# One departure of TensorE per chunk, attention one batch ahead, and a pinned TensorE order

## The chip, the cores and the metric

The program runs on one NeuronCore of a Trainium2 chip. The metric is the device time of one execution in microseconds. The engines are named as in the profile: PE is TensorE, DVE VectorE, ACT ScalarE, POOL GpSimd, SP the engine that issues most DMAs.

## The reference

Eight batches, eight heads, 576 positions, head dimension 64. Three layers follow each other; all of it is float32.

```python
# 1 Nystrom attention, m = 32 landmarks (means of 18 positions)
A, Bm, C = sm(q, k_lm), sm(q_lm, k_lm), sm(q_lm, k)      # softmax of scaled products
Z = Bm.T / (norm1(Bm) * norminf(Bm) + 1e-6)
for _ in range(6): Z = 2*Z - Z @ Bm @ Z                  # inverse of Bm by iteration
x = A @ Z @ C @ v                                        # 4608 tokens x 512
# 2 gated layer: 512 -> 1536 -> 512
x = (silu(x @ w_gate) * (x @ w_val)) @ w_out
# 3 soft mixture of experts, 8 experts x 4 slots
logits = x @ phi
slots  = softmax(logits, over tokens).T @ x
out    = softmax(logits, over slots) @ expert(slots)     # expert: relu(s @ w1) @ w2
```

## The kernel before

**The main loop.** It goes over the 8 batches, and in a batch over 12 chunks `j` of 128 gate columns: 96 chunks. Softmax matrix A stands transposed in SBUF as a high and a low part (EH, EL), and Z C v is folded with the weights into `g`, again as GH and GL. A chunk is 24 matmuls at line 903 (`mm3`): for each half of the positions six into the bank `pg` (gate) and six into `pv` (value). This text calls these 24 the stream. ACT makes `u` of `pg` (silu, L301, or tanh, L917), DVE multiplies `u` and `pv` into `hT` (L932) and transposes `hT` into HB (L761).

**The other matmuls stand between them.** All are plain float32 (the stream is float32r), and most use the array in smaller tiles than the stream's 128*128 (a row names the tile; `m_n`, `m_t` and `m_ps` have 128*128 too): `l`, the logits of the chunk before (L756, 8 records); `g` for two chunks (L710, 16 records; one chunk in batches 0 and 7 and at the end of batch 6), which ACT casts to GH (L727) and DVE subtracts to GL (L741); for the attention of the next batch the landmark sums on DVE (L322), the scores `m_a` of A and `m_c` of C (L529, 16 records for each half), transposes `m_t` (L596, L601), `m_v` (L618), six steps `m_n` of the inverse (L637) and the product `m_w` (L522); for the slots of the batch before `m_dr`, which spreads the weights DN over the row groups (L841), and the slot sums `m_d` (L872, 144 records), added to Sacc by DVE (L882). A row of the profile counts two records for each such matmul.

A stretch of such matmuls between two of the stream is called a departure here.

**What sets their order.** `slot(i)` in `unit` is called four times a chunk (after each six of the stream), so a batch has 48 slots. The lists in SCHED (`at*` attention, `am*` softmax of A, `sm` soft mixture) say in which slot each step of a generator is written, numbers below zero belonging to the batch before. A scheduler then orders the instructions of each engine, and may move a matmul past others. PSUM is shared: three banks `x` for nearly everything beside the stream, two `pg`, two `pv`, one `l`. `in_order` keeps exponentials and silus of ACT in written order, so that tables change twice in a batch; chunks named in TANH use tanh, whose table is that of the exponential.

After the loop the slots go through the experts, whose weights are loaded from batch 7 on, and the output is written.

Of the kernel before, what the change touches and what calls it, by code (L numbers as in the profile page):

```python
# [8 lines left out]
F32 = mybir.dt.float32  # L9
# [44 lines left out]
def nystrom_softmoe_kernel(  # L54
# [286 lines left out]
    def attention_tiles(b):  # L341
        ks = ap.tile([128, 4, M], F32, tag="ks", name="ks")
        qs = ap.tile([128, 4, M], F32, tag="qs", name="qs")
        if b != 1:
            e_tiles(b)
# [3 lines left out]
        return ks, qs, AN, CE  # L349

    def first_attention(side):
        b = 0
        ks, qs, AN, CE = attention_tiles(b)
        NBUF = big("w5", "newton").rearrange("p (i q m) -> p i q m", q=2, m=128)
# [177 lines left out]
    def attention(b):  # L532
        assert b == 1 or ("att", b - 1) in seq
        ks, qs, AN, CE = attention_tiles(b)
        for nm, dst in (("k", ks), ("q", qs)):
            for hp in range(4):
# [3 lines left out]
                yield  # L540
        for half in range(2):
            ms = [psp.tile([128, 512], F32, tag="x", name="m_a", bufs=3) for r in range(2)]
            scores(ms, ks, "q", b, half, range(4))
            assert b == 1 or ("asm", b - 1) in seq
            seq.add(("A", b, half))
            for r in range(2):
                dve.transpose(AN[r][:, 9 * half:9 * half + 9, :], ms[r][:, 0:HALF].rearrange("p (t r) -> p t r", r=32))
                yield
        for half in range(2):
            ms = [psp.tile([128, 512], F32, tag="x", name="m_c", bufs=3) for r in range(2)]  # L550
            scores(ms, qs, "k", b, half, range(4))
            n = HALF
            if half:
                n += M
                for hp in range(4):
                    for r in range(2):
                        pe.matmul(ms[r][32 * hp:32 * hp + 32, HALF:n], qs[64 * r:64 * r + 64, hp, :],
                                  ks[64 * r:64 * r + 64, hp, :], start=True, stop=True)
            for r in range(2):
                act.copy(CE[r][:, HALF * half:HALF * half + n], ms[r][:, 0:n])  # L560
                yield
        if b == 1:
# [101 lines left out]
    def a_softmax(b, qs=(0, 1)):  # L664
        EH, EL = E_t[b]
        AN, mxA = A_t[b]
# [125 lines left out]
    def softmoe(b):  # L792
# [96 lines left out]
        yield  # L889
        dve.tensor_reduce(mx, c, axis=AX.X, op=ALU.add)  # L890
        dve.tensor_scalar(mx, mx, 1e-9, None, ALU.add)
        dve.reciprocal(mx, mx)
        dve.tensor_tensor(out=c, in0=c, in1=bc, op=ALU.mult)
        yield
# [11 lines left out]
    def unit(b, j, slot):  # L906
# [118 lines left out]
    def tail_loads(b, n):  # L1025
# [19 lines left out]
    for a in range(1, nb):  # L1045
# [4 lines left out]
        sm = softmoe(a - 1)  # L1050
        for r in S_["sm"]:
            todo[48 * a + r].append(sm)
    prev = None
    for b in range(nb):
        for j in range(NJ):
            p = prev
            def slot(i):
# [29 lines left out]
                if n == 47:  # L1087
# [211 lines left out]
```

## Time and profile before

| | us |
|---|---|
| median of 3 runs | 687.33 (687.18 to 689.19) |
| profiled execution, its own time | 688.07 |
| its span | 686.3 |
| PE busy | 641.6 (93%) |
| DVE busy | 484.5 (71%) |
| ACT busy | 307.2 (45%) |
| POOL busy | 72.2 (11%) |

The profiled execution is 0.74 us above the median and 1.77 us longer than its span. Busy PE is not PE at work: a matmul that waits inside the array counts. So stretches are measured here from the start of one instruction to the start of another. Batch 0 takes 85.5 us of the loop, in which the weights are prepared too; batches 1 to 6 take 68 to 70 us each, batch 7 57.6 us, and the part after the loop some 85 us. In the stretches of batches 1 to 7 the granted clock is 1.00, that is 2.4 GHz.

### The profile page before, as it was taken

What the parts mean: (1) busy time and instruction counts of PE and PEld (TensorE: products, weight loads), DVE (VectorE), ACT (ScalarE), POOL (GpSimd) and SP (SyncE); (2) the same over time, 40 slices, a digit from 0 to 9 for tenths busy, and PEclk for the clock granted to TensorE, in tenths of its full rate; (3) what the DMA queues carried; (4) which work ended last, traced back from release to release, by engine and by line L of the source; (5) the groups of instructions that cost most, each with busy time, mean ns of one, the idle gap of its engine ahead of it and who ended that gap; (6) DMA issues with size and microseconds to landing.
All of it is one profiled execution on the core that took longest, in us unless ns stands there. A gap on an engine that the chain in (4) does not pass through costs nothing.

```text
span 686.3 us, 18326 instructions
## 1 busy us (share of the span) xinstructions
PE 641.6 (93%) x7639; PEld 470.2 (69%) x7639; DVE 484.5 (71%) x1166; ACT 307.2 (45%) x776; POOL 72.2 (11%) x81
## 2 busy tenths in 40 slices
PE   5699999999999999999999999999999999989991
PEld 2576767776877687777777777777768886843560
DVE  4999989878657985798569856976696655550441
ACT  2566875356335533463246324632364342321441
POOL 0401012012001200120012001200130000010000
PEclk9799999999999999999999999999999999999996
DMA  7788773232203230224022402240212296789999
GB/s 283 258 323 316 279 269 119 83 126 84 70 1 96 72 114 2 72 82 126 1 71 71 140 1 70 72 139 1 71 63 63 77 367 227 249 268 351 348 369 326
DMA packets 59843, 105.01 MB, mean 153 GB/s; under 512 B 3824, under 2 KB 29552, under 8 KB 58224
## 3 DMA queue, kind: packets, MB, share of 16 engines
q1 hardware_dynamic: 59760, 103.84, 45.0%
q8 instruction: 60, 0.98, 0.6%
q14 instruction: 23, 0.19, 0.1%
HBM read 91.24 MB, written 12.58 MB: 151 GB/s over the span
## 4 chain that ended last, share of the span: by engine, by line
PE 68%; DVE 17%; ACT 6%; DMA 4%; issue 2%; POOL 1%; SPq 0%; POOLq 0%; ACTq 0%; DVEq 0%
PE pg L903 20%; PE pv L903 17%; PE g L710 6%; PE l L756 4%; PE m_n L637 3%; PE m_d L872 3%; PE m_f L1232 2%; PE m_f L1184 2%; PE m_a L529 2%; DMA q<-in_qT_dram 2%; DMA v<-in_v_dram 2%; DVE bd L311 2%; DVE GL L741 1%; DVE Sacc L882 1%; DVE qs L322 1%
## 5 line engine op out<-in xcount | busy, mean ns | idle before, releaser
L301 ACT ACTIVATE u<-pg 128x288 f32<-128x288 f32 x174 | 71.4, 411 | 143.8 <-PE pg L903 138.7
L932 DVE TENSOR_TENSOR hT<-u,pv 128x288 f32<-128x288 f32 x174 | 78.2, 450 | 56.9 <-PE pv L903 51.3
L903 PE MATMUL pg<-EH,GH 128*128 128x288 f32 x384 | 96.9, 330 | 2.5 <-ACT GH L727 1.6
L741 DVE TENSOR_TENSOR GL<-g,GH 128x512 fp32r<-128x512 f32 (+1 forms) x122 | 66.0, 571 | 38.7 <-ACT GH L727 38.5
L903 PE MATMUL pv<-EH,GH 128*128 128x288 f32 x384 | 91.2, 312 | 0.5 <-DVE hT L932 0.5
L903 PE MATMUL pg<-EH,GL 128*128 128x288 f32 x384 | 86.0, 299 | 0.0
L903 PE MATMUL pg<-EL,GH 128*128 128x288 f32 x384 | 84.0, 298 | 0.0
L903 PE MATMUL pv<-EH,GL 128*128 128x288 f32 x384 | 83.1, 295 | 0.0
L903 PE MATMUL pv<-EL,GH 128*128 128x288 f32 x384 | 82.7, 296 | 0.0
L727 ACT CAST GH<-g 128x512 fp32r<-128x512 f32 (+1 forms) x122 | 54.2, 496 | 56.4 <-PE g L710 56.3
L903 PEld LDWEIGHTS pg<-EH,GH 128*128 128x128 f32 x384 | 59.9, 189 | 25.3 <-issue 20.3
L761 DVE STREAM_TRANSPOSE HB<-hT 128x576 f32<-128x576 f32 x96 | 73.9, 770 | 1.3
L903 PEld LDWEIGHTS pv<-EH,GH 128*128 128x128 f32 x384 | 61.4, 188 | 18.0 <-issue 16.2
L903 PEld LDWEIGHTS pg<-EH,GL 128*128 128x128 f32 x384 | 62.3, 188 | 2.2 <-issue 2.1
L903 PEld LDWEIGHTS pg<-EL,GH 128*128 128x128 f32 x384 | 61.6, 188 | 1.8 <-issue 1.8
L903 PEld LDWEIGHTS pv<-EL,GH 128*128 128x128 f32 x384 | 61.6, 188 | 0.9 <-issue 0.9
L903 PEld LDWEIGHTS pv<-EH,GL 128*128 128x128 f32 x384 | 61.9, 188 | 0.5 <-issue 0.5
L710 PE MATMUL g<-w,WB 64*32 64x512 f32 (+1 forms) x976 | 56.5, 510 | 0.4 <-ACT WB L523 0.4
L756 PE MATMUL l<-hT,P_sb 128*32 128x128 f32 (+1 forms) x768 | 47.4, 298 | 0.7 <-DVE hT L932 0.6
L756 PEld LDWEIGHTS l<-hT,P_sb 128*32 128x32 f32 x768 | 15.9, 108 | 40.3 <-issue 17.8
L872 PE MATMUL m_d<-HB,HB 32*32 32x384 f32 x1116 | 39.5, 491 | 0.3 <-DVE GL L741 0.3
L683 POOL TENSOR_TENSOR AN<-AN,mxA 128x576 f32<-128x576 f32 x16 | 18.4, 1170 | 179.6 <-DVE mxA L682 163.3
(248 smaller groups left out, 945.2 us busy)
## 6 DMA issues: line engine op xcount, KB each, us to landing
k<-in_kT_dram SPq DMA_DIRECT2D x52, 288.0 KB, 3.8
ffn<-in_w_dram SPq DMA_DIRECT2D x13, 1024.0 KB, 8.7
ffn<-in_w_dram SPq DMA_DIRECT2D x24, 512.0 KB, 8.8
HB<-in_w_cat_dram SPq DMA_DIRECT2D x8, 1024.0 KB, 7.8
v<-in_v_dram SPq DMA_DIRECT2D x8, 1024.0 KB, 6.0
q<-in_qT_dram SPq DMA_DIRECT2D x28, 288.0 KB, 3.2
HB<-in_w_out_dram SPq DMA_DIRECT2D x12, 512.0 KB, 5.8
wr<-in_w_cat_dram SPq DMA_DIRECT2D x4, 1024.0 KB, 9.4
```

Source lines behind the costliest of these rows:

```text
L301: i = act.activation(*a, **kw)
L311: dve.tensor_tensor(out=dst[:, q, :].rearrange("p (h m) -> p h m", h=4), in0=src.unsqueeze(1).to_broadcast([128, 4, 32]), in1=bm3, op=ALU. ...
L637: pe.matmul(m[:, 96 * q:96 * q + 96], bd[:, q, :], RV[:, q, :], start=True, stop=True)
L683: lambda q: pool.tensor_tensor(out=AN[q], in0=AN[q], in1=bc[q], op=ALU.subtract),
L710: pe.matmul(gs[r][32 * hp:32 * hp + 32, 0:256 * n].rearrange("p (u f) -> p u f", u=n), WB[b % 2][64 * r:64 * r + 64, hp, :], w[64 * r:64 * ...
L727: act.copy(H_, g)
L741: dve.tensor_tensor(out=GL, in0=g, in1=GH, op=ALU.subtract)
L756: pe.matmul(L[32 * c:32 * c + 32, 0:32 * k], P_sb[:, j, :], main[:, 0:k, c, :], start=j == 0, stop=j == NJ - 1)
L761: dve.transpose(HB[b % 2][:, S * j:S * j + S].rearrange("p (t r) -> p t r", r=32), hT[:, 0:S].rearrange("p (t r) -> p t r", r=32))
L872: pe.matmul(ms[a][32 * g:32 * g + 32, 0:384].rearrange("p (j f) -> p j f", j=NJ), d_of(a, g, k), hb[32 * a:32 * a + 32, :, 4 * k + g, :], ...
L903: pe.matmul(ps[:, 0:HALF], G_t[b, j, q, sel_][h], e[:, q, ts_], start=n == 0, stop=n == 5)
L932: dve.tensor_tensor(out=o, in0=u, in1=pv[:, 0:HALF], op=ALU.mult)
```

## The change

- The scores of A for all four tiles (two halves, two rows of heads) are issued together, so too those of C; they take one bank `pv` and the three `x` (from batch 2 on, `together`).
- Attention of batch b+1 begins in batch b-1 (`at3`, `am3`): landmark sums in its slots 29 to 40, scores of A in slot 41; the rest follows in batch b. The tiles EH and EL are asked for later, where A is transposed back.
- The steps are put into slots 4j+1, in which the logits stand.
- DN is spread by 12 small DMAs on SP in place of four matmuls and four copies, for batches 0 to 5.
- `keep_order` ties each PE instruction from batch 1 on to the one written before it.
- The tanh chunks are others (three halves of a batch as before); the first `g` of a batch stands one slot earlier; two fences hold a few DVE reductions back.

```diff
-    'at3': [-3, -2, -1, 0, 3, 4, 5, 6, 8, 8, 10, 10, 16, 16, 18, 18, 19, 20, 20, 21, ...
+    'at3': [-19, -18, -17, -16, -11, -10, -9, -8, -7, -6, -6, -5, 1, 2, 2, 3, 4, 5, 5, 6, ...
-    'sm': [1, 3, 10, 17, 19, 20, 23, 24, 24, 27],
+    'sm': [1, 2, 3, 6, 7, 7, 25, 26, 26, 28],
...
+    def keep_order(engine, start, end):
+        last = None
+        for i in nc.cur_bb.bb.instructions[start:end]:
+            if i.engine == engine:
+                if last is not None:
+                    tc.add_manual_dep(i, last.name, mybir.DependencyInfo(
+                        mybir.DependencyClass.NoSync, mybir.DependencyReason.DATA), reason="keep_order")
+                last = i
...
+        def score_tiles(name):
+            ms = [psp.tile([128, 512], F32, tag="pv" if i == 3 else "x", name=name, bufs=2 if i == 3 else 3)
+                  for i in (3, 0, 1, 2)]
+            return {(1, 1): ms[0], (0, 0): ms[1], (0, 1): ms[2], (1, 0): ms[3]}
...
+            if together:
+                t = score_tiles(name)
+                for half in (1, 0):
+                    product(half, [t[half, 0], t[half, 1]])
+                for half, r in ((1, 1), (0, 0), (0, 1), (1, 0)):
+                    eviction(half, r, t[half, r])
+                    yield
...
-            for g in range(4):
+            for i in range(1, 4 if b < nb - 2 else 1):
+                for a in range(4):
+                    sp.dma_start(DR[32 * a:32 * a + 32, a ^ i], DN[32 * (a ^ i):32 * (a ^ i) + 32])
+            for g in range(4 if b == nb - 2 else 0):
                 m = psp.tile([128, 512], F32, tag="x", name="m_dr", bufs=3)
...
-            d_of = lambda a, g, k: DR[32 * a:32 * a + 32, g, k, :]
+            d_of = lambda a, g, k: (DN if a == g else DR[:, g])[32 * a:32 * a + 32, k, :]
...
-    TANH = {(4, 1), (5, 0), (5, 1)}
+    TANH = [{(5, 0), (5, 1), (6, 0)}, {(1, 1), (2, 0), (2, 1)}]
...
-                if n == 46 and b + 1 < nb:
+                if n == (46 if b == 0 else 45) and b + 1 < nb:
                     g_unit(b + 1, 0)
...
+    keep_order(mybir.EngineType.PE, middle, n_ins())
```

By the built programs, PE leaves the stream 227 times in the loop before and 139 times with the change; in each of batches 2 to 5 it is 28 times and 12 times.

On PE, the end of batch 3 before (`pg` and `pv` are the stream; inverse step, product `m_w`, logits, `g` of the next batch):

```order
L637 MATMUL m_n<-RV,bd 128x96 x2
...
L522 MATMUL m_w<-bd,VD 64x128 x2
...
L756 MATMUL l<-hT,P_sb 32x160 x2
L756 MATMUL l<-hT,P_sb 32x128 x2
...
L710 MATMUL g<-w_214,WB_75 32x512 x8
...
L756 MATMUL l<-hT,P_sb 32x160
L903 MATMUL pg<-EH,GL 128x288
L903 MATMUL pv<-EH,GL 128x288
L756 MATMUL l<-hT,P_sb 32x160
L756 MATMUL l<-hT,P_sb 32x128 x2
```

With the change the same place reads:

```order
L945 MATMUL pv<-EH,GL 128x288 x2
L794 MATMUL l<-hT,P_sb 32x160 x2
L794 MATMUL l<-hT,P_sb 32x128 x2
L534 MATMUL m_w<-bd,VD 64x128 x2
L541 MATMUL m_a<-q_0_4419,ks 32x288 x2
...
L541 MATMUL m_a<-q_3_4425,ks 32x288 x2
L945 MATMUL pg<-EH,GH 128x288 x2
...
L794 MATMUL l<-hT,P_sb 32x160 x2
L794 MATMUL l<-hT,P_sb 32x128 x2
L748 MATMUL g<-w_214,WB_75 32x512 x8
```

`m_w` and the scores of A (eight matmuls for each half, of the batch after the next) stand behind the logits in one departure, and `g` behind the next logits; the logits that were cut in two are whole.

On PE, the slot sums in batch 3 before (`m_dr` spreads DN, `m_d` are the sums):

```order
L841 MATMUL m_dr<-DN,cst 128x160 x3
L903 MATMUL pv<-EH,GH 128x288
L841 MATMUL m_dr<-DN,cst 128x160
L903 MATMUL pv<-EH,GH 128x288
...
L903 MATMUL pv<-EH,GL 128x288 x2
L872 MATMUL m_d<-HB_84,HB_85 32x384 x72
L903 MATMUL pg<-EH,GH 128x288 x2
```

With the change:

```order
L794 MATMUL l<-hT,P_sb 32x160 x2
L794 MATMUL l<-hT,P_sb 32x128 x2
L913 MATMUL m_d<-HB_84,DN 32x384
L913 MATMUL m_d<-HB_84,HB_85 32x384 x4
...
L913 MATMUL m_d<-HB_84,HB_85 32x384 x2
L672 MATMUL m_n<-RV,bd 128x96 x2
L945 MATMUL pg<-EH,GH 128x288 x2
```

`m_dr` has gone, `m_d` stands behind the logits, and an inverse step follows it directly.

On DVE, batch 3 before, the landmark sums (`ks`, `qs`) and GL:

```order
L882 SCALAR_TENSOR_TENSOR Sacc<-Sacc,al,m_d 128x384 x4
L322 TENSOR_REDUCE ks<-k_0_3986 128x32
...
L322 TENSOR_REDUCE ks<-k_1_3988 128x32
...
L322 TENSOR_REDUCE ks<-k_3_3992 128x32
...
L322 TENSOR_REDUCE qs<-q_0_4644 128x32
L322 TENSOR_REDUCE qs<-q_1_4646 128x32
L322 TENSOR_REDUCE qs<-q_2_4648 128x32
L741 TENSOR_TENSOR GL<-g,GH 128x512 x2
```

With the change, in batch 3:

```order
L923 SCALAR_TENSOR_TENSOR Sacc<-Sacc,al,m_d 128x384 x2
L322 TENSOR_TENSOR bd<-m_n,cst 128x128 x2
L923 SCALAR_TENSOR_TENSOR Sacc<-Sacc,al,m_d 128x384
...
L923 SCALAR_TENSOR_TENSOR Sacc<-Sacc,al,m_d 128x384
...
L333 TENSOR_REDUCE ks<-k_0_3789 128x32
...
L333 TENSOR_REDUCE ks<-k_1_3791 128x32
L333 TENSOR_REDUCE ks<-k_2_3793 128x32
...
L779 TENSOR_TENSOR GL<-g,GH 128x512
...
L779 TENSOR_TENSOR GL<-g,GH 128x512
...
L333 TENSOR_REDUCE ks<-k_3_3795 128x32
```

Three of the landmark sums now stand between the additions to Sacc and the two GL of the pair of chunks that comes next; the last four (`qs`) stand further on, ahead of the next pair's GL. Before, the GL of such a pair stood behind seven.

## Rows read from the trace of the kernel before

**Rows 1.** Busy time by engine (count), batch 3; then PE's granted clock, DMA.

```profile
266.10:336.03 69.93, 68.66 (x834) 52.12 (x833) 53.30 (x129) 30.69 (x80) 8.25 (x8) 1.00 0.23 69
```

**Rows 2.** Timeline, PE, batch 4: start, time, engine, line, tiles, shape, count, [idle].

```profile
345.53 0.42 PE L903 MATMUL pg<-EL,GH 128*128 128x288 f32 x2
345.79 0.43 PE L903 MATMUL pg<-EH,GL 128*128 128x288 f32 x2
346.15 0.71 PE L529 MATMUL m_a<-q,ks 64*32 64x288 f32 x16
346.79 0.53 PE L903 MATMUL pv<-EH,GH 128*128 128x288 f32 x2
347.16 0.42 PE L903 MATMUL pv<-EL,GH 128*128 128x288 f32 x2
```

**Rows 3.** Timeline, PE, about the start of batch 4.

```profile
334.11 1.09 PE L710 MATMUL g<-w,WB 64*32 64x512 f32 x16
335.13 0.53 PE L903 MATMUL pv<-EH,GH 128*128 128x288 f32 x2
...
337.68 0.46 PE L756 MATMUL l<-hT,P_sb 128*32 128x160 f32 x2
338.07 0.40 PE L903 MATMUL pg<-EH,GL 128*128 128x288 f32 x1
```

**Rows 4.** Timeline, PE, middle of batch 4.

```profile
361.92 0.55 PE L841 MATMUL m_dr<-DN,cst 32*128 32x160 f32 x6
...
363.35 0.40 PE L903 MATMUL pv<-EH,GH 128*128 128x288 f32 x1
...
367.39 5.03 PE L872 MATMUL m_d<-HB,HB 32*32 32x384 f32 x144
```

**Rows 5.** Timeline, PE, batch 7.

```profile
571.15 4.32 PE L872 MATMUL m_d<-HB,HB 32*32 32x384 f32 x144
```

**Rows 6.** Timeline, PE, end of batch 4.

```profile
386.80 0.66 PE L637 MATMUL m_n<-RV,bd 128*128 128x96 f32 x4 [0.38 <-ACT RV L644]
...
388.90 0.58 PE L637 MATMUL m_n<-RV,bd 128*128 128x96 f32 x4
389.26 0.51 PE L903 MATMUL pg<-EH,GH 128*128 128x288 f32 x2
...
391.03 1.09 PE L710 MATMUL g<-w,WB 64*32 64x512 f32 x16
392.05 0.47 PE L756 MATMUL l<-hT,P_sb 128*32 128x160 f32 x8
392.45 0.69 PE L637 MATMUL m_n<-RV,bd 128*128 128x96 f32 x4
392.92 0.52 PE L903 MATMUL pg<-EH,GH 128*128 128x288 f32 x2
...
396.73 0.47 PE L756 MATMUL l<-hT,P_sb 128*32 128x160 f32 x8
397.12 0.54 PE L903 MATMUL pg<-EH,GH 128*128 128x288 f32 x2
...
400.06 0.44 PE L522 MATMUL m_w<-bd,VD 128*64 128x128 f32 x4 [0.37 <-POOL bd L659]
```

**Rows 7.** Groups by line and form: count, busy us, mean ns, idle before.

```profile
L741 DVE TENSOR_TENSOR GL<-g,GH 128x512 fp32r<-128x512 f32 x70 | 46.1, 685 | 30.1 <-ACT GH L727 29.9
...
L301 ACT ACT_TABLE_LOAD x20 | 25.7, 1283 | 1.2 <-DVE stat L574 0.9
...
L322 DVE TENSOR_REDUCE qs<-q 128x32 f32<-128x576 f32 x28 | 20.6, 743 | 7.0 <-DMA q<-in_qT_dram 6.9
...
L727 ACT CAST GH<-g 128x512 fp32r<-128x512 f32 x70 | 37.5, 587 | 37.6 <-PE g L710 37.6
...
L301 ACT ACTIVATE CE<-CE,stat 128x576 f32<-128x576 f32 x14 | 10.9, 777 | 6.8 <-DVE stat L574 6.8
```

**Rows 8.** Timeline, DVE, batch 4.

```profile
373.83 2.18 DVE L882 SCALAR_TENSOR_TENSOR Sacc<-Sacc,al,m_d 128x384 f32<-128x384 f32 x4
```

More of the change, by code (lines that the diff above doesn't have):

```diff
@@ L348, in attention_tiles, with landmark_tiles @@
         CE = [ap.tile([128, S + M], F32, tag=f"CE{q}", name=f"CE{q}") for q in range(2)]
-        return ks, qs, AN, CE
+        return AN, CE
+    def landmark_tiles():
+        return ap.tile([128, 4, M], F32, tag="ks", name="ks"), ap.tile([128, 4, M], F32, tag="qs", name="qs")
     def first_attention(side):
         b = 0
-        ks, qs, AN, CE = attention_tiles(b)
+        ks, qs = landmark_tiles()
+        e_tiles(b)
+        AN, CE = attention_tiles(b)
         NBUF = big("w5", "newton").rearrange("p (i q m) -> p i q m", q=2, m=128)
@@ L532, in attention @@
     def attention(b):
-        assert b == 1 or ("att", b - 1) in seq
-        ks, qs, AN, CE = attention_tiles(b)
+        assert b == 1 or ("q", b - 1) in seq
+        ks, qs = landmark_tiles()
         for nm, dst in (("k", ks), ("q", qs)):
@@ L540, in attention @@
                 yield
[L541 to L550, printed above, removed]
+        def score_tiles(name):
+            ms = [psp.tile([128, 512], F32, tag="pv" if i == 3 else "x", name=name, bufs=2 if i == 3 else 3)
+                  for i in (3, 0, 1, 2)]
+            return {(1, 1): ms[0], (0, 0): ms[1], (0, 1): ms[2], (1, 0): ms[3]}
@@ L551, in attention, with a_eviction, c_product @@
+        together = b > 1
+        assert b == 1 or ("v", b - 1) in seq and ("asm", b - 1) in seq
+        AN, CE = attention_tiles(b)
+        def a_eviction(half, r, m):
+            dve.transpose(AN[r][:, 9 * half:9 * half + 9, :], m[:, 0:HALF].rearrange("p (t r) -> p t r", r=32))
+            if (half, r) == (1, 0 if together else 1):
+                seq.add(("A", b, 1))
+        def c_product(half, ms):
             scores(ms, qs, "k", b, half, range(4))
-            n = HALF
             if half:
-                n += M
@@ L555, in attention, with c_eviction @@
                 for hp in range(4):
                     for r in range(2):
-                        pe.matmul(ms[r][32 * hp:32 * hp + 32, HALF:n], qs[64 * r:64 * r + 64, hp, :],
+                        pe.matmul(ms[r][32 * hp:32 * hp + 32, HALF:HALF + M], qs[64 * r:64 * r + 64, hp, :],
                                   ks[64 * r:64 * r + 64, hp, :], start=True, stop=True)
-            for r in range(2):
-                act.copy(CE[r][:, HALF * half:HALF * half + n], ms[r][:, 0:n])
-                yield
+        def c_eviction(half, r, m):
+            n = HALF + M * half
+            act.copy(CE[r][:, HALF * half:HALF * half + n], m[:, 0:n])
@@ new lines, in attention @@
+        for name, product, eviction in (
+                ("m_a", lambda half, ms: scores(ms, ks, "q", b, half, range(4)), a_eviction),
+                ("m_c", c_product, c_eviction)):
+            if together:
[5 more added lines that the diff above has]
+                    yield
+            else:
+                for half in range(2):
+                    ms = [psp.tile([128, 512], F32, tag="x", name=name, bufs=3) for r in range(2)]
+                    product(half, ms)
+                    for r in range(2):
+                        eviction(half, r, ms[r])
+                        yield
@@ L573, in attention @@
             dve.tensor_scalar(stat[:, q, 2:3], stat[:, q, 0:1], -SC / SEG, None, ALU.mult)
-            dve.tensor_scalar(stat[:, q, 3:4], stat[:, q, 1:2], -SC / (SEG * SEG), None, ALU.mult)
+            i = dve.tensor_scalar(stat[:, q, 3:4], stat[:, q, 1:2], -SC / (SEG * SEG), None, ALU.mult)
+            fence["stat"] = getattr(i, "ins", i)
             yield
@@ L673, in inv @@
             mx = mxA[:, q, :]
-            dve.tensor_reduce(mx, AN[q], axis=AX.X, op=ALU.add)
+            with tc.issue_after(fence["stat"]) if b > 1 else nullcontext():
+                dve.tensor_reduce(mx, AN[q], axis=AX.X, op=ALU.add)
             dve.tensor_scalar(mx, mx, 1e-9, None, ALU.add)
@@ L679, in back @@
             at[q] = ap.tile([128, S], F32, tag="AT", name="AT", bufs=2)
+            if b not in E_t:
+                e_tiles(b)
             dve.transpose(at[q].rearrange("p (t r) -> p t r", r=32), AN[q])
@@ L687, in a_softmax @@
                   back,
-                  lambda q: act.copy(EH[:, q, :], at[q]),
-                  lambda q: pool.tensor_tensor(out=EL[:, q, :], in0=at[q], in1=EH[:, q, :], op=ALU.subtract)):
+                  lambda q: act.copy(E_t[b][0][:, q, :], at[q]),
+                  lambda q: pool.tensor_tensor(out=E_t[b][1][:, q, :], in0=at[q], in1=E_t[b][0][:, q, :],
+                                               op=ALU.subtract)):
             for q in qs:
@@ L889, in softmoe @@
         yield
[L890 to L893, printed above, removed]
+        with tc.issue_after(fence["sum"]):
+            dve.tensor_reduce(mx, c, axis=AX.X, op=ALU.add)
+            dve.tensor_scalar(mx, mx, 1e-9, None, ALU.add)
+            dve.reciprocal(mx, mx)
+            dve.tensor_tensor(out=c, in0=c, in1=bc, op=ALU.mult)
         yield
@@ L913, in unit @@
             u = mp.tile([128, HALF], F32, tag="u", name="u", bufs=2)
-            by_tanh = (j, half) in TANH and 0 < b < nb - 1
+            by_tanh = 0 < b < nb - 1 and (j, half) in TANH[b > 1]
             if by_tanh:
@@ L1031, in tail_loads @@
         if b == last:
-            if n == 25:
+            if n == 26:
                 for t in range(NW, NW + 3):
@@ L1050, in nystrom_softmoe_kernel @@
         sm = softmoe(a - 1)
-        for r in S_["sm"]:
+        for r in S_["sm1" if a == 1 else "sm"]:
             todo[48 * a + r].append(sm)
     prev = None
+    n_ins = lambda: len(nc.cur_bb.bb.instructions)
     for b in range(nb):
+        if b == 1:
+            middle = n_ins()
         for j in range(NJ):
@@ L1084, in slot @@
                         next(gen, None)
-                if n == 46 and b + 1 < nb:
+                if n == (46 if b == 0 else 45) and b + 1 < nb:
                     g_unit(b + 1, 0)
-                if n == 47:
+                if n == (47 if b == 0 else 46):
                     g_low()
             prev = (b, j, *unit(b, j, slot))
+    keep_order(mybir.EngineType.PE, middle, n_ins())
     in_order("exp", warm, one, AF.Exp)
```

5 lines of the change are left out of this document (removed), and 9 rows, old and new, of the table SCHED.

## The prediction

> **What bounds the kernel now.** I read the busy times by stretch first, one stretch for each batch. In batch 3 [rows 1] PE is busy for 68.66 of 69.93 us at full granted clock, DVE for 53.30, ACT for 30.69. So PE sets the pace, and the question is what its 70 us consist of. For that I went down its timeline and measured from start to start. Two matmuls of the stream start 0.26 to 0.27 us after the two before them [rows 2], 133 ns each. A batch has 12 x 24 = 288 of them, 38.3 us. The other 31.6 us are the 28 departures, so each of those has to be priced, and in the stretches of batches 1 to 7 nothing else is left over.
>
> A departure costs more than its own matmuls. In [rows 2] the last two of the stream start at 345.79, the next could start at 346.055, and `m_a` starts at 346.15: 0.095 to leave. From `m_a` to the stream it is 0.64, and the first pair behind it takes 0.37 in place of 0.265: 0.105 to come back. Together 0.84 for one `m_a`. `g` takes 1.02 from its start to the stream [rows 3] and also 1.02 from its start to the logits behind it (391.03 to 392.05 in [rows 6]); the logits take 0.39 to the stream alone (396.73 to 397.12) and 0.40 to what follows them in a departure (392.05 to 392.45). So where one of these stands beside another, one leaving and one return are saved: 0.2 us. Where two of the same shape stand together more is saved: `m_a` and `g` have 16 records each, of 288 and 512 columns, and the 0.38 between 0.64 and 1.02 is 1.7 ns a column. So 288 columns cost 0.49 themselves, and a second `m_a` directly behind the first costs 0.49 in place of 0.84, 0.35 less.
>
> **The change part by part**, for one of the batches 2 to 5:
>
> - `m_dr` goes. Its two pieces [rows 4] last from 361.92 to 363.35, with one matmul of the stream between them: 1.43 + 0.095 + 0.105 - 0.13 = 1.50 us saved. Its four copies go from ACT and DVE. Its 12 DMAs are issued in slot 7 and wanted in slot 25, four chunks or some 20 us later; on SP they stand among loads that have as long. I price them at nothing.
> - The logits that were cut in two at the batch's start: half of them costs 0.39 to the stream (337.68 to 338.07 in [rows 3]), as much as the whole. One departure less, 0.59.
> - `m_a` and `m_c` in one piece each: 2 x 0.35 = 0.70.
> - Five joints of unlike shapes that were two departures: logits with `m_w`, `m_w` with `m_a`, logits with `m_c`, with `g`, with `m_d`: 5 x 0.2 = 1.0.
> - `m_n` behind the logits brings nothing. Alone it takes 0.36 to the stream (388.90 to 389.26), behind the logits 0.47 (392.45 to 392.92) [rows 6]: what the logits save in coming back, it pays on changing shape. The transposes are of the same kind; I take 0 for both (bounds 0 and 0.2 each, `m_n` four times).
> - Waits that end because a step has a chunk more to ripen: `m_d` spans 5.03 us in batch 4 and 4.32 in batch 7 [rows 4, 5], for the same 144 records; in batch 4 it stands half a chunk behind `g` and waits for that one's banks, with the change a whole chunk: 0.7. `m_n` waited 0.38 for ACT and `m_w` 0.37 for POOL [rows 6]: 0.8 together. Sum 1.5.
>
> That is 5.3 us a batch. Against it stand new waits, since PE's order is now fixed and the steps are clustered. None of them is in the trace, so I work out three places from durations.
>
> First, `m_n` directly behind `m_d`. All three banks `x` hold `m_d`, so `m_n` waits until DVE has added the first to Sacc. Four additions take 2.18 us [rows 8], one some 0.6; with the passing on at both ends, less what a change of shape costs anyhow: 0.75 (bounds 0.5, and 2.2 if all four come first).
>
> Second, GL behind landmark sums on DVE, chunks 6 to 8. From `m_n` on, PE reaches the last GL that it needs after half a chunk, a chunk with its departure of `g`, logits and `m_n` (2.05) and a chunk's half and more: 1.6 + 1.6 + 2.05 + 1.6 + 0.65 = 7.5 us. In that time DVE has, in the new order, three Sacc (1.6), four bd and two RV (1.2), two hT and an HB (1.4), small ones of the slots (0.6), three landmark sums (2.0, 742 ns each less the overlap with the next, which is 0.08 by four Sacc in 2.18) and two GL (1.2; 685 ns each) [rows 7, 8]: 8.0. So 0.5 to 0.6 late (bounds 0 and 2, the latter with full durations and no overlap).
>
> Third, all exponentials of a batch now fall in slots 5 to 7, where `g` of the second pair is cast. In the new order of ACT a table load (1.28) and the exponentials of one CE (0.78, some 0.3 more for its small part) stand ahead of the two casts (0.59 each), and GL (0.69) comes behind [rows 7]. Counted from the maximum of CE, which DVE can have 5.7 us into the batch, GL is there at 10.7, and PE wants it at 10.4: 0.3 (bounds 0 and 1).
>
> With 1.65 of such waits the net is 3.6 us a batch, for four batches 14.4.
>
> The other batches differ. Batch 6 loses its two `m_a`, which are done earlier (1.68), `m_dr` (1.5), one `m_c` joint (0.35), four joints (0.8) and the wait of `m_d` (0.7): 5.0, less 1.05 of waits, as it has no landmark sums: 3.9. Batch 1 gets the `m_a` of two batches, in two departures beside logits: 2 x (0.84 + 0.49 - 0.2) = 2.26 for 1.68, so 0.6 more; it loses `m_dr`, a joint of `m_c`, two other joints, the waits of `m_d` and `m_w` (1.5 + 0.35 + 0.4 + 0.7 + 0.4 = 3.35), and I put 2.0 of waits on it, since DVE gets eight landmark sums more there: 0.7 gained. Batch 7 has `m_d` beside logits: 0.2. Batch 0 is in the order of before. The part after the loop follows loads that start when batch 6 ends, so it moves with that, and I keep its length.
>
> Sum 14.4 + 3.9 + 0.7 + 0.2 = 19.2. The profiled execution took 688.07: 668.9. The median of the runs is 0.74 lower: 668.
>
> **The rivals.**
>
> *No new wait.* The scheduler's order on DVE and ACT could just fit, as before: there too seven landmark sums stood ahead of a pair of GL, and PE did not wait for it. Then 1.65 x 4 + 1.05 + 2.0 = 9.7 more are gained: 658.
>
> *A change of shape costs as much as leaving.* For `m_n` it does [rows 6]. If so for all joints of unlike shapes, 1.0 a batch is lost in four, 0.8 in batch 6, 0.4 in batch 1, 0.2 in batch 7: 5.4, so 673. Against it speak the 1.02 of `g` with and without logits behind it; the joints of `m_w` and `m_d` are not in these rows. The Trainium skill (TensorEngine Tiling (Array Packing), section Tiling Modes, Key Properties) states that changing the tiling mode, and not just the tile, drains the engine; by that rule nothing but joints of one shape and the waits would pay, which is this rival. The trace agrees for `m_n` (0.47 against 0.36) and agrees only in part for `g` and logits, where 0.2 is saved.
>
> *Twice the waits.* DVE was busy for 53.3 us of 70 and has now 66; batch 1 more. If a batch waits 3.3 us: 678.
>
> *Slower.* One mechanism: PE cannot pass over a `pg` whose GH or GL is late, and both engines that make these have clusters ahead of them. If the casts come behind all exponentials (a load 1.28, two CE and two of A, which has as many columns, 4 x 0.78) PE stops for 4.4 us at chunk 2; if all eight landmark sums stand ahead of one pair's GL, five more are 3.3; with `m_n` it is 8.4 a batch, 3.1 more than is gained: 688 + 12 = 700. It decides from 5.3 us a batch on. Against it: the built order has one CE and three landmark sums ahead, and the casts had 37.6 us of idle before them [rows 7], so they do not start from a queue.
>
> **How the numbers follow.** Forecast 668 (its own range 662 to 673) 0.45; no new wait 0.13; shape changes at full price 0.15; twice the waits 0.15; waits that just eat the gain, about 687, 0.05; slower 0.07. A difference under 0.3%, 2 us, can hardly be told from none. Faster 0.88, within 0.05, slower 0.07. The range that leaves out 2 in 10 goes from the first rival to a little above doubled waits: 657 to 680.
>
> **What would show it.** Batches 2 to 5 at 66.2 us each in place of 69.2 to 70.0, with 12 departures; no `m_dr` before batch 7; `m_d` at 4.3 us without idle in it; `m_n` behind it idle for 0.7 by a Sacc; the first `pg` of chunk 8 idle for half a us by GL; batch 1 hardly shorter; the part after the loop as long as before. It is wrong if PE's idle by GH, GL or Sacc comes to over 3 us a batch, if joints such as `m_w` with `m_a` save nothing, or if the last part grows by what the loop lost.

## The result, and the profile after

The changed kernel takes 676.56 us, median of 4 runs (674.40 to 678.34), against 687.35 for the kernel before, whose runs were taken beside it: ratio 0.9836, interval [0.9802, 0.9869]. The profiled execution took 674.40, its span is 672.6; the three others ran at a lower mean granted clock (0.975 to 0.980 against 0.984, by estimate some 5 to 12 us more at half clock) and were 1.8 to 3.9 us longer.

Where the time went is read by batches, from the first matmul of the stream in one to the first in the next. Busy time by engine in batches 1, 3, 6, 7 and in the part after the loop, first after the change, with the columns of [rows 1]:

```profile
125.93:200.28 74.35, 70.78 (x862) 53.21 (x859) 54.86 (x131) 31.50 (x82) 10.59 (x10) 0.98 0.28 86
...
266.17:332.08 65.91, 64.80 (x826) 51.01 (x825) 51.78 (x127) 29.06 (x77) 8.45 (x8) 1.00 0.25 77
...
463.88:527.74 63.86, 63.11 (x810) 50.59 (x809) 44.92 (x115) 28.97 (x79) 6.16 (x6) 1.00 0.12 39
527.74:588.12 60.38, 58.06 (x713) 45.80 (x712) 33.37 (x75) 21.36 (x57) 0.12 (x1) 1.00 0.78 262
588.12:672.60 84.48, 65.33 (x726) 35.08 (x724) 28.62 (x80) 24.48 (x58) 4.71 (x11) 0.93 1.03 336
```

and the same stretches of the kernel before, but for batch 3, which is [rows 1]:

```profile
126.10:196.36 70.26, 69.01 (x838) 52.22 (x835) 50.32 (x126) 32.21 (x84) 8.26 (x8) 1.00 0.22 70
...
475.21:543.28 68.07, 67.99 (x850) 52.09 (x849) 49.08 (x123) 30.84 (x82) 8.25 (x8) 1.00 0.15 50
543.28:601.02 57.74, 57.34 (x713) 45.53 (x712) 33.64 (x77) 21.00 (x57) 0.12 (x1) 1.00 0.79 274
601.02:686.30 85.28, 65.18 (x726) 35.01 (x724) 28.98 (x80) 24.46 (x58) 4.69 (x11) 0.94 1.02 334
```

Batches 2 to 5 each take 65.9 us and are shorter by 3.85, 4.02, 3.32 and 4.06, together 15.25; batch 6 is 4.2 shorter, the last part 0.8. But batch 1 is 4.1 us longer and batch 7 2.6. With 0.2 at the start that is 13.7, the difference of the two profiled executions. Two batches out of eight gave back 6.7 of the 20.4 us won. The 0.8 of the last part need not be the change's: in the traces of the experiments below, which leave its instructions as they are, that part takes 83.5 to 85.9.

The steady batches look as the prediction said: 12 departures, no `m_dr`. PE's timeline in batch 3, to be held against [rows 2, 3]:

```profile
304.53 0.69 PE L672 MATMUL m_n<-RV,bd 128*128 128x96 f32 x4 [0.65 <-DVE Sacc L923]
...
312.45 0.29 PE L945 MATMUL pg<-EH,GL 128*128 128x288 f32 x1
313.11 0.40 PE L945 MATMUL pg<-EH,GL 128*128 128x288 f32 x1 [0.38 <-DVE GL L779]
...
323.70 0.47 PE L794 MATMUL l<-hT,P_sb 128*32 128x160 f32 x8
324.10 0.44 PE L534 MATMUL m_w<-bd,VD 128*64 128x128 f32 x4
324.46 1.20 PE L541 MATMUL m_a<-q,ks 64*32 64x288 f32 x32
325.60 0.53 PE L945 MATMUL pg<-EH,GH 128*128 128x288 f32 x2
...
328.97 0.47 PE L794 MATMUL l<-hT,P_sb 128*32 128x160 f32 x8
329.37 1.09 PE L748 MATMUL g<-w,WB 64*32 64x512 f32 x16
330.38 0.53 PE L945 MATMUL pg<-EH,GH 128*128 128x288 f32 x2
```

Three operations follow each other in 0.40, 0.36 and 1.14 us. `m_n` behind `m_d` waits for the first Sacc. In chunk 8 the second of the `pg` by GL starts 0.66 after the first, in place of 0.133, and the next pair is 0.10 late: 0.63. These are the waits that the prediction looked for.

Batch 1 shows something else. PE's timeline about `m_d`, SP's in the same stretch, and busy time by engine in the 3.3 us behind the standstill:

```profile
157.07 0.83 PE L913 MATMUL m_d<-HB,DN 32*32 32x384 f32 x2
158.22 1.36 PE L913 MATMUL m_d<-HB,HB 32*32 32x384 f32 x4 [0.33 <-ACT CT L632]
161.87 0.51 PE L913 MATMUL m_d<-HB,HB 32*32 32x384 f32 x2 [2.28 <-DMA HB<-DN]
...
163.31 0.84 PE L913 MATMUL m_d<-HB,DN 32*32 32x384 f32 x1
```

```profile
152.03 0.33 SPq L160 DMA_DIRECT2D q<-in_qT_dram  x1
152.77 7.81 SPq L879 DMA_DIRECT2D HB<-DN  x12
160.68 4.07 SPq L160 DMA_DIRECT2D q<-in_qT_dram  x3
```

```profile
163.00:166.30 3.30, 3.30 (x85) 2.30 (x80) 2.72 (x5) 0.00 (x0) 1.34 (x1) 0.50 0.46 138
```

SP needs 7.81 us for the 12 issues, one after the other, the last at 160.0; between 158.22 and 161.87 PE starts no more than the four records of the second row and is idle for the last 2.28 us. Then the granted clock, the third number from the end, is 0.50 for 3.4 us, 1.2 GHz, and an `m_d` takes 0.84 in place of 0.50. Batch 7, PE's timeline:

```profile
536.19 0.42 PE L945 MATMUL pv<-EH,GL 128*128 128x288 f32 x2
538.53 0.55 PE L882 MATMUL m_dr<-DN,cst 32*128 32x160 f32 x6 [1.92 <-DVE DN L867]
539.48 0.53 PE L882 MATMUL m_dr<-DN,cst 32*128 32x160 f32 x2 [0.40 <-DVE HB L885]
539.94 0.54 PE L945 MATMUL pg<-EH,GH 128*128 128x288 f32 x2
...
560.14 0.83 PE L913 MATMUL m_d<-HB,DN 32*32 32x384 f32 x2
560.79 0.85 PE L913 MATMUL m_d<-HB,HB 32*32 32x384 f32 x5
...
565.34 0.54 PE L945 MATMUL pg<-EH,GH 128*128 128x288 f32 x2
```

Here `m_dr` is still a matmul; it stands in slot 7 with the transpose of DN that it reads, and PE waits for it. `m_d`, directly behind `g` and logits, takes 5.20 to the stream; before, from 571.15 [rows 5] to 575.40, it took 4.25. The 0.40 is no new wait; the kernel before has it in batch 7 too:

```profile
566.91 0.53 PE L841 MATMUL m_dr<-DN,cst 32*128 32x160 f32 x2 [0.40 <-DVE HB L844]
```

### The profile page after: what moved, and what is told of

Its sections match the earlier page's. It is cut to its first block, busy times and chain, and to the rows that moved or that the text cites. A ratio compares the mean times of both kernels' runs of the same rounds, so it can differ in the third digit from the quotient of the medians.

```text
span 672.6 us, 18315 instructions
## 1 busy us (share of the span) xinstructions
PE 623.9 (93%) x7591; PEld 465.8 (69%) x7591; DVE 478.0 (71%) x1154; ACT 298.8 (44%) x764; POOL 73.3 (11%) x81
## 5 line engine op out<-in xcount | busy, mean ns | idle before, releaser
L945 PE MATMUL pg<-EH,GH 128*128 128x288 f32 x384 | 93.9, 324 | 2.6 <-ACT GH L765 1.6
L945 PE MATMUL pv<-EH,GH 128*128 128x288 f32 x384 | 84.0, 298 | 0.0
L945 PE MATMUL pg<-EL,GH 128*128 128x288 f32 x384 | 83.5, 296 | 0.0
L794 PE MATMUL l<-hT,P_sb 128*32 128x160 f32 (+1 forms) x768 | 45.2, 298 | 0.8 <-DVE hT L974 0.6
L913 PE MATMUL m_d<-HB,DN 32*32 32x384 f32 x288 | 37.7, 514 | 0.0
```

The costliest lines, as they stand in the source:

```text
L794: pe.matmul(L[32 * c:32 * c + 32, 0:32 * k], P_sb[:, j, :], main[:, 0:k, c, :], start=j == 0, stop=j == NJ - 1)
L913: pe.matmul(ms[a][32 * g:32 * g + 32, 0:384].rearrange("p (j f) -> p j f", j=NJ), d_of(a, g, k), hb[32 * a:32 * a + 32, :, 4 * k + g, :], ...
L945: pe.matmul(ps[:, 0:HALF], G_t[b, j, q, sel_][h], e[:, q, ts_], start=n == 0, stop=n == 5)
```

## The experiments

All ratios are to the kernel before on the same chip. Times of batches come from the profiled execution of each kernel, measured as above.

**1. Batch 1's m_d four slots later.**

```diff
-    'sm1': [1, 2, 4, 19, 20, 21, 24, 25, 25, 28],
+    'sm1': [1, 2, 4, 19, 20, 21, 28, 29, 29, 32],
```

> Edit: only in batch 1, m_d and the steps behind it come four slots later (slot 28 in place of 24); the copies of DN that it reads are issued in slot 21 as before, so they get about 5.5 us more to land. Theory (PE stands in front of m_d for those copies, and the granted clock falls after this standstill): batch 1's departure with m_d falls from 10.6 us to 4.3 to 5.0, the stretch at half clock at 163 to 166 us goes, batch 1 takes 68.0 to 69.0 us in place of 74.35, and the time is 5 to 6.5 us shorter, 668 to 671. Rival A (batch 1 is long because DVE has the landmark sums of two batches, and the wait only moves to GL, GH or Sacc): batch 1 stays over 72 us and the time gains less than 2 us. Rival B (the clock falls by itself there, whatever PE did ahead of it): the wait goes but m_d still takes 0.8 us or the stream some 3 us more at half clock, and the gain is 3 to 4 us.

Measured: 670.99 us, ratio 0.9745 [0.9719, 0.9772]. Batch 1 takes 70.17, its departure with `m_d` 4.63, and the clock stays at 1.00 in it: rival A falls, and of B nothing is seen. It is still 1.2 to 2.2 us above the expectation; `m_n` now waits 1.6 us for RV, since DVE, ahead of RV, has stood for 3.6 us in front of a landmark sum whose `q` had not landed (DVE's timeline):

```profile
171.46 0.75 DVE L333 TENSOR_REDUCE qs<-q 128x32 f32<-128x576 f32 x1 [3.56 <-DMA q<-in_qT_dram]
```

And batch 7, which the edit doesn't touch, is 63.30 instead of 60.38. The same 1.92 us standstill in front of `m_dr` was followed there by a fall of the clock (busy time by engine in that stretch; half clock lasted 6.8 us):

```profile
535.20:542.00 6.80, 6.62 (x42) 4.72 (x43) 1.57 (x5) 2.77 (x6) 0.00 (x0) 0.50 1.05 387
```

**2. Batch 7's soft mixture in its old slots.**

```diff
+    'sm7': [1, 3, 10, 17, 19, 20, 23, 24, 24, 27],
...
-        for r in S_["sm1" if a == 1 else "sm"]:
+        for r in S_["sm1" if a == 1 else "sm7" if a == nb - 1 else "sm"]:
```

> Edit: only in batch 7, the steps of the soft mixture stand in the slots that they had in the kernel before, so that m_dr is no longer in the slot of DN's transposes and m_d no longer in a slot with g. Theory (m_dr waits 1.9 us for DVE's DN, and m_d beside g waits for the banks that g has just filled): batch 7 falls from 60.39 to 57.6 to 58.2 us, the rest is unchanged, and the time is 2.2 to 2.8 us shorter. Rival (batch 7 is longer for work of the attention or of the last part that now falls there, not for these two steps): batch 7 stays over 60 us, gain under 0.5 us.

Measured: 672.24, ratio 0.9756 [0.9737, 0.9775]. Batch 7 takes 57.73, as before the change; batch 1 still has its standstill and 3.4 us at half clock, and at 73.90 it is 0.45 shorter, for which no cause was looked for. The 2.6 us of batch 7 are these two steps. The time is 4.3 us shorter, more than the 2.2 to 2.8 expected. Half clock behind the standstill in front of `m_dr`, which goes too and cost 2.9 us in experiment 1, would explain it; no trace shows it for the other executions of the changed kernel.

**3. Both edits.**

> Edit: the two edits together, batch 1's m_d four slots later and batch 7's soft mixture in its slots of before. Theory: the two losses are apart from each other and add up, 7.5 to 9 us, so that the time is 666 to 669 and its ratio to the kernel before about 0.971. Rival (what is won in batch 1 is lost again in batch 7 or in the last part, which follow loads): under 5 us gained.

Measured: 666.74, ratio 0.9680 [0.9656, 0.9703]. They add up: 9.8 us below the changed kernel, a little more than expected. The profiled execution, 669.89, was the longest of five; in it the wait of `m_n` for RV in batch 1 was 2.0 us, half clock followed (175.1 to 178.5), and batch 1 took 72.14.

**4. Scores by halves again.**

```diff
-        together = b > 1
+        together = False
```

> Edit on the changed kernel: the scores m_a and m_c of batches 2 to 7 are again made half by half, in two departures each, nothing else. Prediction's term: a second piece of the same shape behind the first saves 0.35 us, so 2 x 0.35 x 6 attentions = 4.2 us are lost, with batches 2 to 5 at 66.6 us in place of 65.9 and 14 departures each. Rival (a second piece of one shape saves nothing beyond the 0.2 us of one leaving and one return): 2.4 us lost. Rival (PE's saving is taken back by waits for the banks, since the larger product needs four at once): nothing lost or even a gain.

Measured: 676.77, ratio 0.9818 [0.9796, 0.9840]; the times can't tell it from the changed kernel, whose interval it overlaps. The batches can: batches 2 to 4 take 66.43 in place of 65.9, 0.52 to 0.54 more, with 14 departures, and over all batches 2.9 us are lost: between the 4.2 of the prediction's term and the 2.4 of the first rival; the last rival falls. PE's timeline in batch 3:

```profile
324.97 0.72 PE L541 MATMUL m_a<-q,ks 64*32 64x288 f32 x16
325.62 0.53 PE L945 MATMUL pg<-EH,GH 128*128 128x288 f32 x2
...
326.61 0.71 PE L541 MATMUL m_a<-q,ks 64*32 64x288 f32 x16
327.26 0.53 PE L945 MATMUL pv<-EH,GH 128*128 128x288 f32 x2
```

One piece of `m_a` takes 0.65, two behind each other 1.14 (324.46 to 325.60 above): the second costs 0.49, and by itself 0.84. That is the 0.35 of the prediction, and more than one leaving and one return. For `m_c` the two departures cost 2.14 together (logits included) against 1.99 in one: 0.15 only. Together they are 0.51 of the 0.52 to 0.54.

**5. m_d by itself, two slots later** (on both slot edits, as are 6 to 8).

```diff
-    'sm': [1, 2, 3, 6, 7, 7, 25, 26, 26, 28],
+    'sm': [1, 2, 3, 6, 7, 7, 27, 28, 28, 30],
```

> Base: the kernel with both slot edits (e3_both, 666.7). Edit: in batches 2 to 6 m_d and the steps behind it come two slots later, in slot 27, so that m_d departs by itself and m_n, in slot 25, stands directly behind the logits. Prediction's term: m_n behind m_d waits 0.75 us for the first Sacc, so this goes and one leaving and one return (0.2) come: 0.55 a batch in five batches, batches 2 to 5 at 65.35 in place of 65.9 with 13 departures, time 2.5 to 3 us shorter. Rival (the wait only hid other lateness: the next m_n or GL is late instead): batches at 65.9 to 66.3, no gain.

Measured: 665.23, ratio 0.9685 [0.9664, 0.9706]; against 0.9680 of the kernel that it starts from no gain can be read from the times. The batches show it: 2 to 5 take 65.17 on average instead of 65.92, with 13 departures, a little more than expected. The last part, which the edit doesn't touch, is 1.3 us longer in the profiled execution. Batch 1 is 69.89 with the clock at 1.00.

**6. PE's order not pinned.**

```diff
-    keep_order(mybir.EngineType.PE, middle, n_ins())
```

> Base: e3_both. Edit: PE's order is not pinned, nothing else; the scheduler then puts four to six matmuls of the stream between m_d and m_n, takes late halves of pg in another order in the chunk, and leaves the clusters as they are. Theory (the 1.65 us of new waits a batch come from the fixed order, and matmuls of the stream can fill them): the 0.7 by Sacc and the 0.9 in the stream go, 0.2 to 0.4 is paid for m_n standing alone, batches 2 to 5 at 64.6 to 65.0 us, time 4 to 5 us shorter. Rival (the order is worth its price: free, the steps drift apart as before and waits return elsewhere): batches at 65.9 to 67 and the time the same or up to 4 us longer.

Measured: 662.13, ratio 0.9621 [0.9608, 0.9634], 4.6 us below its base, as expected. Batch 3 takes 64.93 (busy time by engine), and PE's timeline shows what now lies between `m_d`, whose last matmul starts ahead of these rows, and `m_n`:

```profile
259.73:324.66 64.93, 64.84 (x826) 51.05 (x825) 51.46 (x127) 29.19 (x77) 8.42 (x8) 1.00 0.25 79
```

```profile
297.37 0.54 PE L946 MATMUL pg<-EH,GH 128*128 128x288 f32 x2
297.75 0.43 PE L946 MATMUL pg<-EL,GH 128*128 128x288 f32 x2
298.01 0.43 PE L946 MATMUL pg<-EH,GL 128*128 128x288 f32 x2
298.28 0.58 PE L673 MATMUL m_n<-RV,bd 128*128 128x96 f32 x4
298.64 0.51 PE L946 MATMUL pv<-EH,GH 128*128 128x288 f32 x2
```

Six matmuls of the stream fill the time that DVE needs for Sacc: the wait of 0.65 is gone, and `m_n` alone costs 0.44, no more than behind logits. Of the 0.9 in the stream 0.3 went, not all of it.

**7. DN's copies issued from two queues.**

```diff
-    sp.dma_start(DR[32 * a:32 * a + 32, a ^ i], DN[32 * (a ^ i):32 * (a ^ i) + 32])
+    (pool if a % 2 else sp).dma_start(DR[32 * a:32 * a + 32, a ^ i], DN[32 * (a ^ i):32 * (a ^ i) + 32])
```

> Base: e3_both. Edit: of the 12 copies of DN in each batch, the six to the odd partition groups are issued by POOL, six by SP as before. Theory (SP needs 0.59 to 0.65 us to issue each copy, 7.8 us for the twelve, and holds up the loads of q that DVE's landmark sums and, behind them in DVE's order, RV wait for): in batch 1 SP is busy with the copies for about 3.8 us, q lands some 4 us earlier, m_n no longer waits 1.6 to 2.0 us for RV, and batch 1 comes to 68 to 70 us in place of 72.1 (70.2 without the stretch at half clock); the steady batches stay within 0.3 us. Rival (RV is late because DVE has the sums of two attentions, not for the loads): batch 1's wait for RV stays at 1.6 or more.

Measured: 667.44, ratio 0.9700 [0.9687, 0.9713]: not told apart from its base in time. Batch 1 is 69.12, its wait for RV 0.5; against 70.17 of experiment 1, which had full clock too, 1.05 gained. The rival falls: RV was late for the loads.

**8. Batch 1 as before the change, with m_dr on PE.**

```diff
-    'sm1': [1, 2, 4, 19, 20, 21, 28, 29, 29, 32],
+    'sm1': [1, 3, 10, 17, 19, 20, 23, 24, 24, 27],
...
-            for i in range(1, 4 if b < nb - 2 else 1):
+            for i in range(1, 4 if 0 < b < nb - 2 else 1):
...
-            for g in range(4 if b == nb - 2 else 0):
+            for g in range(4 if b in (0, nb - 2) else 0):
```

> Base: e3_both. Edit: in batch 1 alone the soft mixture of batch 0 is as in the kernel before: its slots, and DN spread by m_dr on PE with four copies, in place of the 12 DMAs. Theory (batch 1's loss comes from the 12 copies issued one after the other on SP): no wait over 0.6 us at m_dr or m_d, m_dr costs 1.5 us, batch 1 takes 69 to 70.5 us, no half clock in it, and the time is 1.5 to 3 us shorter. Rival (batch 1 is crowded anyway, by two attentions): batch 1 stays at 72 or more.

Measured: 672.32, ratio 0.9767 [0.9753, 0.9780]: 5.6 us longer than its base. The expectation failed. Batch 1 takes 73.44, at full clock. Who waited for whom on PE in it (total, times, longest, us):

```profile
PE m_dr L883 <- DVE HB L886: 1.5, 1, 1.5
PE m_t L632 <- ACT Sacc L927: 1.2, 1, 1.2
```

The copies of `m_dr` are late on DVE, and in these slots `m_t` is written directly behind `m_d`, whose banks `x` it needs: 8.6 us for the two in one departure, against 4.6 and 1.5 apart in experiment 1. So the old way isn't free in this batch either: a pinned order that puts two users of the same banks side by side costs 2.5 us here. Against the 70.17 of experiment 1, also at full clock, the batch is 3.3 longer; the rest of the 5.6 is not located. By itself this run does not say what the 12 issues cost; experiment 12 does.

**9. The changed kernel, not pinned.** The edit is that of 6, on the kernel as changed.

> Base: the changed kernel as it is (676.6). Edit: PE's order is not pinned, nothing else. Theory (fixed order costs 1.0 us in each of batches 2 to 5, 0.75 in batch 6, and nothing to speak of in batches 1 and 7, whose waits come from the 12 copies and from DN): batches 2 to 5 at 64.9, batch 1 at 72.5 to 74, batch 7 at 60.4, time 670.5 to 672.5. Rival (with the slots of the change the pin keeps batch 1 or 7 from becoming worse still): batch 1 or 7 grows by 1 us or more, time 674 or above.

Measured: 666.57, ratio 0.9687 [0.9671, 0.9703]: 10 us below the changed kernel, 4 more than expected. Batches 2 to 5 are 64.9, as said, but batch 1 came to 71.43 and batch 7 to 58.79. Unpinned, one matmul of the stream stands inside `m_d` of batch 1, its departures come to 8.6 us instead of 10.7, and no half clock follows; in batch 7 `m_dr` is put among the next logits and has no wait left but 0.4 us for a bank. I had held both waits to be out of the scheduler's reach.

**10. All three: slot edits, no pin, two queues.**

> Edit: the two slot edits, no pin, and DN's copies from two queues, together. Theory (each takes away a wait of its own): batches 2 to 5 at 64.9, batch 1 at 68.0 to 68.8, batch 7 at 57.8, no stretch at half clock before the last part, time 660.5 to 662.5. Rival (POOL's issues delay bd or GL that PE then waits for): batches 2 to 5 over 65.3, time 663 to 666.

Measured: 661.76, ratio 0.9614 [0.9599, 0.9630], with batches 1, 3 and 7 at 68.30, 64.92 and 57.74 and no half clock before the last part. It beats both kernels, 14.8 us below the changed one; of experiment 6 (0.9621) it can't be told apart.

**11. No attention a batch ahead.**

```diff
-    'at3': [-19, -18, -17, -16, -11, -10, -9, -8, -7, -6, -6, -5, 1, 2, 2, 3, 4, 5, 5, 6, 7, 8, 9, 9, 9, 11, 13, 17, 21, 25, 29, 33, 37, 41],
+    'at3': [-3, -2, -1, 0, 3, 4, 5, 6, 9, 10, 10, 11, 17, 18, 18, 19, 19, 20, 20, 21, 21, 22, 23, 23, 23, 25, 27, 29, 31, 33, 35, 37, 39, 42],
-    'am3': [-4, -3, -3, -2, 6, 7, 9, 10, 11, 12, 14, 15, 17, 18, 19, 20, 22],
+    'am3': [12, 12, 13, 13, 20, 21, 22, 23, 24, 25, 27, 29, 31, 32, 34, 36, 37],
```

> Base: the changed kernel. Edit: attention and its softmax of batches 3 to 7 keep the slots of batch 2's, so that none begins a batch ahead; the rest, the pin included, stays. Prediction's terms: batch 1 has the m_a and m_c of one batch less (1.7 to 3.6 us shorter, with less on DVE), batch 6 gets them (1.7 to 2.1 us longer), and in batches 2 to 5 what a longer lead saved (the waits of m_n and m_w, 0.8 a batch) comes back: 66.5 to 67.5, time 676 to 682. Rival (the lead is worth more: the clusters of DVE and ACT fall on one batch's chain): batches 2 to 5 at 69 or more, time 688 or above. Rival (the lead is worth nothing): batches at 65.9, time 674 to 676.

Measured: 698.34, ratio 1.0150 [1.0132, 1.0169]: the first rival. Batches 2 to 5 take 70.2 to 70.8 and have 18 departures, since several steps stand where no logits do. Who waited on PE in batches 0 to 7:

```profile
PE l L794 <- DVE hT L974: 5.0, 5, 1.0
PE m_t L631 <- ACT CE L312: 4.4, 6, 0.9
PE m_n L672 <- ACT RV L679: 2.9, 6, 0.5
PE m_n L672 <- DVE RV L688: 2.6, 9, 0.3
```

About 15 us of such waits: with one batch for the whole chain and PE's order fixed, these steps of it are waited for. Six departures and waits together are the 4.3 to 4.9 us a batch. The lead and the joints can't be had apart with these lists, so this run prices the two together.

**12. The changed kernel, with two queues.** The edit of 7 on the kernel as changed: `m_d` of batch 1 stays in slot 24, the order stays pinned.

> Base: the changed kernel as it is, m_d of batch 1 in slot 24 and PE's order pinned. Edit: six of the 12 copies of DN are issued by POOL, six by SP. Theory (m_d in batch 1 waits because the 12 issues stand in one row on SP: the last at 160.0, landed at 161.8): with six on each queue the last is issued at about 156.5 and landed at about 158.5, m_d stands still for about 0.3 us in place of 3.6 and its departure takes 5.0 to 7.2 us in place of 10.6, no stretch at half clock follows, batch 1 comes to 68.8 to 71 us and the time to 670.5 to 673, batch 7 unchanged at 60.4. Rival (m_d's other conditions, CT and the banks, are as late as the copies): the departure stays over 8.5 us and the gain under 2 us.

Measured: 671.25, ratio 0.9774 [0.9758, 0.9789]. PE's matmuls stand in the same order as in the changed kernel. Batch 1's timeline of PE, then SP's and POOL's, then busy time by engine in batch 1:

```profile
156.40 0.83 PE L913 MATMUL m_d<-HB,DN 32*32 32x384 f32 x2
157.56 0.83 PE L913 MATMUL m_d<-HB,HB 32*32 32x384 f32 x4 [0.33 <-ACT CT L632]
157.89 0.51 PE L913 MATMUL m_d<-HB,DN 32*32 32x384 f32 x1
```

```profile
152.10 3.74 SPq L879 DMA_DIRECT2D HB<-DN  x6
```

```profile
152.69 3.11 POOL L879 DMA_DIRECT2D HB<-DN  x6 [10.87 <-PE g L748]
```

```profile
125.25:194.84 69.59, 68.29 (x862) 52.19 (x859) 54.77 (x131) 31.29 (x82) 13.72 (x16) 1.00 0.29 91
```

From the second `m_d` row to the third it is 0.33 in place of 3.65, the departure 5.88 in place of 10.69, the clock 1.00, batch 1 69.59 in place of 74.35; batch 7 stays at 60.37. This settles batch 1: the row of 12 issues on SP is the cause, 3.3 us as PE's wait and 1.5 by the half clock behind it. The whole profiled execution is only 4.1 shorter, since its last part is 1.4 longer; with two queues (experiments 7, 10 and 12) that part takes 85.6 to 85.8, inside the spread given above, and whether the queues have a share in it is not shown.

## Why the prediction was right, and where it was not

The forecast was 668, the result 676.6: inside the range and faster as said, but above the 662 to 673 of its likeliest case. That it lies beside the 678 of the rival with twice the waits is chance: the three new waits of a steady batch come to 1.67 us, where 1.65 was said, so that rival and the one without new waits both fall there, and the missing time lies elsewhere. Its working for the steady batches held in nearly every term; two batches that it treated in a sentence each did not.

What a steady batch gained (us; "apart" and "joined" departures are measured from the last matmul of the stream before to the first behind, less 0.133, with the late first pair):

| term of the prediction | said | measured |
|---|---|---|
| `m_dr` gone | 1.50 | 1.48 (its two departures in batch 3 of before) |
| logits not split | 0.59 | 0.58 |
| second piece of `m_a` | 0.35 | 0.355 (experiment 4) |
| second piece of `m_c` | 0.35 | 0.15 (experiment 4) |
| logits with `m_w` with `m_a` | 0.40 | 0.39 (0.20 for `m_w`, which stands alone in batch 1: 2.09 against 1.72 + 0.57) |
| logits with `m_c`, with `g`, with `m_d` | 0.60 | 0.19, 0.20 and 0.18 (experiments 4, before, 5 against 6) |
| `m_n`, `m_t` with logits | 0 | 0.00 and 0.00 (1.03 against 0.59 + 0.44; 1.64 against 1.64) |
| wait of `m_d` ends | 0.7 | 0.59 in batch 3, 0.7 in the others |
| waits of `m_n`, `m_w` end | 0.8 | 1.4 in batch 3 |
| `m_n` behind `m_d` | -0.75 | -0.73 |
| GL in chunk 8 | -0.6 | -0.63 |
| GH, GL in chunk 2 | -0.3 | -0.31 |
| net | 3.6 | 3.3 to 4.1, mean 3.8 |

Two terms missed on opposite sides: the second piece of `m_c` was put 0.2 too high, the waits of `m_n` and `m_w` in batch 3 were put 0.6 too low.

The rival of the full shape change falls for all joints but those that the prediction itself set to 0. The Trainium skill (TensorEngine Tiling (Array Packing), section Tiling Modes, Key Properties) says that a change of the tiling mode drains the engine and gives no price for it. The rows agree in part: where the next operation is `m_n` or `m_t` on the whole array nothing is saved, between the smaller tiles 0.18 to 0.20 is.

Batch 6 was said to become 3.9 shorter and became 4.2 shorter; the last part was to stay and is 0.8 shorter, which is inside its spread.

**The step that failed** is the price of `m_dr`'s substitute: "Its 12 DMAs are issued in slot 7 and wanted in slot 25, four chunks or some 20 us later ... I price them at nothing." That is so for the list `sm` and holds in batches 2 to 6. Batch 1 has a list of its own, `sm1`, in which the copies are issued in slot 21 and `m_d` stands in slot 24, four us later, and 12 issues need 7.8 us on SP. Experiment 12 gives batch 1 without this wait: 69.59, that is 0.67 less than before, and 0.7 was predicted. So the forecast for batch 1 missed by this one term, 4.8 us. That the rest of its sum came out is in part luck: in experiment 12 the departure with `m_d` takes 5.88, where the kernel before has 5.58 and 0.7 was to be gained, and the waits of `m_n` come to 1.2, where 2.0 was put for all waits.

In batch 7 the prediction counted only a joint (0.2 gained) and said "no `m_dr` before batch 7", without asking where it stands there. It is written in slot 7 with the transpose of DN; before, they stood a slot apart. That wait (1.92; the departure with `m_dr` takes 3.60 in place of 1.61) and `m_d` in one departure with `g`, whose banks it needs (6.38 in place of 4.44 + 1.27 apart), are the 2.6 us that experiment 2 gives back. With both batches at their measured size the sum is 668.9 + 4.8 + 2.8 = 676.5 for the profiled execution; the 2.1 down to the 674.4 that it took are batches 2 to 5 (0.85), batch 6 (0.3), the last part (0.8) and the start (0.2). The median lies another 2.2 above the profiled execution; that part stays open here.

**What was not asked at all** is what the pin costs. The prediction took the new waits as the price of the new order; Sacc's wait and a third of what is lost in the stream are the price of `keep_order`. Left to the scheduler, the same lists give 64.9 a batch and shorten batches 1 and 7 as well (experiment 9): 10 us, nearly as much as the whole change brought. What of the 0.6 left in the stream comes from which of the clusters was not tried.

The slower rival had its place right (casts behind exponentials, GL behind landmark sums) and the mechanism was there, at a fifth of the price that it needed. Experiment 11 shows that a shorter lead is enough to reach its side, but by waits for hT, CE and RV, not for GH or GL.

## What to carry to other kernels

Price a change for every batch that has a list of its own, the first and last above all: the terms of the steady batch were within some tenths of a us, and the whole miss lay in two batches that were not followed step by step. Small DMAs in place of matmuls are not free on the queue that issues them; count issues times the time of one, and look how many slots lie between the first issue and the reader. Before an order is pinned, run it unpinned: a scheduler that may move independent work into a wait hides what a fixed order makes PE stand for.

## What the runs showed of the hardware

- A copy of 32 partitions from SBUF to SBUF took 0.589 us to issue on SP (median of 12 in batch 1) and some 0.50 on POOL, and landed 1.8 to 2.2 us later (medians), so in the row of 12 on SP the issues (7.81 us) take longer than the landing of the last (1.8).
- Between 30 us and the last part the granted clock fell to half only behind an idle stretch of PE: behind the 2.1 to 2.3 us in front of `m_d` in batch 1 in all four profiled executions that had it (the changed kernel, experiments 2, 4 and 11), behind 2.0 us in front of `m_n` in experiment 3, and behind the 1.92 in front of `m_dr` in batch 7 in two (experiments 1 and 11) and not in three (the changed kernel, experiments 4 and 12). Where no idle stretch was over 1.6 us (the kernel before and experiments 5 to 10) it stayed at 1.00. It stayed at half for 3.4 or 6.8 us; 3.4 cost 1.5 in batch 1, 6.8 cost 2.9 in batch 7. So a wait of 2 us can cost more than twice what the list of waits shows, and not in every execution.
- Why the second piece of `m_c` saves 0.15 and that of `m_a` 0.35, at the same tile and columns, stays open; `m_c` has 16 records of 32 columns between its two pieces in the changed kernel.
